# Attention with its value products cut into quarters of the query columns, and row-max products that take two spare banks in turn

## The chip, the cores and the metric

The kernel runs on one core of a Trainium2 chip. The metric is the time of one launch in device microseconds (us), the median of several runs. The profile comes from one execution taken by the hardware profiler; its engines are PE (matrix products), PEld (the loading of the stationary operand, beside PE), DVE (vector), ACT (activation functions), POOL and SP (here only an issuer of DMAs). PSUM, where matrix products land, has eight banks of 512 fp32 columns on 128 partitions; the kernel holds all eight as one tile `bk`, and `bk[:, 6]` is bank 6.

## What is computed

A gated mix of multi-head attention and of an MLP, both on the same rows:

```python
qkv = (x @ wqkv).reshape(B, S, 3, H, Dh)           # B=1, S=2048, D=448, H=16, Dh=28
scores = einsum("bhqd,bhkd->bhqk", q, k) * Dh ** -0.5
a = einsum("bhqk,bhkd->bhqd", softmax(scores), v)  # then to B,S,D and @ wo
y = layernorm(x)
b = gelu(y @ w1 + b1) @ w2 + b2                    # F = 1792
g = sigmoid((x * gate_w).sum(-1, keepdims=True))
return g * a + (1 - g) * b                         # 2048 x 448, fp32
```

## The kernel before

**Three stages.** First come the projections to queries, keys and values and the layer norm, then the MLP, both in an order that a planner with costs and due times works out (class `Strips`, its products on L472), and from about 455 us on the attention, whose order on PE is written out by hand. The change touches only the attention. Most products are split: an fp32 factor becomes a high and a low part, and three products of parts make one product of full accuracy.

**Row maxima.** The softmax subtracts a bound for each query row that comes from a pass of its own: 1024 products of 28x128 queries by 28x512 keys (`RowMax.one`, L198), each followed by a maximum over its 512 columns on DVE (L200, `mx`). Some of the 1024 are done while the planner runs; the rest are placed one by one between the products of the attention by `lone(s, b, turn)`, where `s` picks one of four heads and `b` the bank of `bk` that the product lands in. The maximum is then an additional row of the score product (29 rows instead of 28).

**Units, groups and turns.** A unit is the 128 keys x 512 queries block of one head: three score products (L1087) into one bank, an exp over the bank (L1090), and its share in a value product. A group has 64 units, 16 key tiles by 4 heads, and there are 16 groups: 4 sets of 4 heads, each with 4 chunks of 512 queries. The 1024 units are taken in turns. `turn_of(u, turn)` issues the score products and exps of one turn: five units while row maxima are owed, and six otherwise, which makes 154 turns of five, 42 of six and a last one of two. Units 0 to 2 of a turn use banks 0 to 2 and one exp (128x1536), the others banks 3, 4 (and 5) and a second exp. The exps write tiles `p0` and `p1` of a pool with three buffers each. The products run as the three parts p = 0, 1, 2 of the first half and then those of the second half. In front of some of these six places stands a `lone`: in a turn of five units in front of places 0, 3 and 5, with banks 6, 5 and 6; in a turn of six in front of 0 and 5, both with bank 6 (bank 5 then holds a unit).

**Value products.** After the scores of a turn the main loop issues value products. One batch (`batch`, L1098) is a key tile of a group: four products side by side, one per head, each of 128 keys x 32 value columns (stationary) by 128 x 512 exps, into 32 rows each of bank 7, which collects a whole group (`start` at key tile 0, `stop` at the last). One of the value columns holds ones, so that the sums of the exps come out beside the products. A batch is issued once its four units were issued in an earlier turn. With five units per turn most turns have one batch, and about every fourth has two; with six they alternate between one and two. `batch` takes an exp out of `prob` as it uses it.

**Group ends.** When a group's last batch is issued, `valued` copies bank 7 to SBUF (`finish_a`, DVE, L958), and two and four turns later the division by the sums follows (`finish_b`, `finish_c`). The batches of that turn stop there. In the last set of heads, `tail` holds the output projection of each finished 128-row tile: `project` (products on L936 to L938, bank 6; the sum with the MLP's part on DVE, `put`, L943), at most one per turn, at the end of a turn.

**Queues and agenda.** Loads and splits for the next group are put down for given turns by `at(turn, fn)` and run from `agenda` between a turn's scores and its values. Their DMAs go out on SP's and other queues, and their arithmetic goes to POOL and DVE. PE's order is that of the program text as it runs.

**The end.** After the last scores (turn 196) comes turn 197 with no scores: the first nine of the twelve projection products of one output tile in bank 6, then the value batches that are left, and `finish_last`, which closes the last group with products against `sel` (L994) and an identity (L1000) and the other projections.

Of the kernel before, what the change touches and what calls it, by code (L numbers as in the profile page):

```python
# [15 lines left out]
P = 128  # L16
# [7 lines left out]
NC = S // CH  # L24
NT = S // P
# [10 lines left out]
def kernel(ctx: ExitStack, tc: tile.TileContext, xt, wqk, wv, wo, xk, w1, b1, w2, b2,  # L36
                          ident_d, sel_d, out):
    nc = tc.nc
# [35 lines left out]
    bk = banks.tile([P, 8, CH], F32, name="bk")  # L74
# [313 lines left out]
    class Strips:  # L388
# [28 lines left out]
        def at(self, t, fn, **uses):  # L417
            self.tasks.append((t, self.count, fn, uses))
            self.count += 1
# [349 lines left out]
    khi, klo, vg = {}, {}, {}  # L769
# [87 lines left out]
    for b, m in enumerate((0, 3, 4)):  # L857
        x = QK(0, m)
# [95 lines left out]
    def finish_a(n):  # L954
        ob = ao.tile([P, CH], F32, name="ob")
        lt = ao.tile([P, CH // 32], F32, name="lt")
        obs[n] = ob, lt
        nc.vector.tensor_copy(ob, pv)  # L958
        nc.sync.dma_start(lt, ob[DH:P:32, :])

    def finish_b(n):
        ob, lt = obs[n]
        rc = ao.tile([P, CH], F32, name="rc")
        obs[n] = ob, rc
        nc.vector.reciprocal(lt, lt)
        r = rls[n]
        nc.sync.dma_start(r.rearrange("j (a b) -> (j a) b", b=CH // 32), lt)
        for j in range(4):
            nc.sync.dma_start(rc[32 * j:32 * j + 32], r[j].partition_broadcast(32))

    def finish_c(n):
        g, c = divmod(n, NC)
        ob, rc = obs.pop(n)
        if g < NG - 1:
            nc.gpsimd.tensor_mul(ot[g][:, c * CH:(c + 1) * CH], ob, rc)
            return
        nc.gpsimd.tensor_mul(ob, ob, rc)
        split_o(g, c, ob)

    def finish_last(n):  # L980

        g, c = divmod(n, NC)
        ob = ao.tile([P, CH], F32, name="ob")
        rc = ao.tile([P, CH], F32, name="rc")
        lt = ao.tile([P, CH // 32], F32, name="lt")
        h, l = (t[:, g] for t in ohs[c])
        tiles = [slice(i * P, (i + 1) * P) for i in range(TPC)]
        po = [bk[:, (6, 0, 1, 2)[i], :D] for i in range(TPC)]
        sums, ways = bk[:, 4, :NG * TPC], bk[:, 5]
        for sl in tiles:  # L990
            nc.scalar.activation(ob[:, sl], pv[:, sl], AF.Copy)
        products(po[1], c * TPC + 1, range(NG - 1))
        for i, sl in enumerate(tiles):
            nc.tensor.matmul(sums[:, NG * i:NG * i + NG], ob[:, sl], sel, start=True, stop=True)  # L994
        nc.vector.reciprocal(lt, sums)
        spread = lt.rearrange("p (i j) -> p i j", j=NG).unsqueeze(3).broadcast_to([P, TPC, NG, 32])
        nc.vector.tensor_copy(rc.rearrange("p (i j d) -> p i j d", j=NG, d=32), spread)
        products(po[2], c * TPC + 2, range(NG - 1))
        for sl in tiles:
            nc.tensor.matmul(ways[:, sl], rc[:, sl], ident, start=True, stop=True)  # L1000
        products(po[3], c * TPC + 3, range(NG - 1))
        for sl in tiles:
            nc.vector.tensor_mul(ob[:, sl], ob[:, sl], ways[:, sl])
            nc.scalar.activation(h[:, sl], ob[:, sl], AF.Copy)
            nc.vector.tensor_sub(l[:, sl], ob[:, sl], h[:, sl].bitcast(F32))
        for i in range(TPC):
            products(po[i], c * TPC + i, (NG - 1,))
            put(po[i], c * TPC + i)

    def begun(n, turn):  # L1010

        g, c = divmod(n, NC)
        if n + 1 < NG * NC:
            for j in range(4):
                at(turn + 1 + j // 2, lambda j=j: fetch_qq(n + 1, j))
            at(turn + 5, lambda: split_qq(n + 1))
            at(turn + 7, lambda: load_ms(n + 1))
        if c == (0 if g == 0 else 2) and g < NG - 1:
            for j in range(4):
                at(turn + 2 + j, lambda j=j: fetch_kk(g + 1, j))  # L1020
                at(turn + 8 + j, lambda j=j: split_kk(g + 1, j))
            at(turn + 13, lambda: key_row(g + 1))
            for t in range(2):
                at(turn + 9 + t, lambda t=t: load_v(g + 1, slice(8 * t, 8 * t + 8)))
        if g == NG - 1:
            for i in range(TPC):
                at(turn + 7 + i, lambda i=i: fetch_acc(c, i))
                at(turn + 9 + i // 2, lambda i=i: weigh_acc(c, i))
            for x in range(NG - 1):
                at(turn + 4 + x, lambda x=x: split_o(x, c, ot[x][:, c * CH:(c + 1) * CH]))  # L1030

    def valued(n, turn):

        g, c = divmod(n, NC)
        if n == NG * NC - 1:
            finish_last(n)
            return
        finish_a(n)
        at(turn + 2, lambda: finish_b(n))
        at(turn + 4, lambda: finish_c(n))  # L1040
        if g == NG - 1:
            for i in range(TPC):
                tail.append((turn + 6 + i, c * TPC + i))

    UNITS = NG * NC * 64
    prob, tail = {}, []
# [3 lines left out]
    def lone(s, b, turn):  # L1050
        if not rowmax.ready(s) or turn < cold[s]:
            return
        for kind, n, j in rowmax.one(s, bk[:, b]):
            if kind == "q":
                at(turn + 1, lambda n=n, j=j: rowmax.load_q(n, j))
            elif kind == "k":
                at(turn + 1, lambda n=n, j=j: rowmax.load_k(n, j))
                cold[j] = turn + 4
            else:
                at(turn + 1, lambda n=n: rowmax.close(n))  # L1060
                at(turn + 2, lambda n=n: rowmax.store(n))

    def turn_of(u, turn):

        left = UNITS - u
        owed = rowmax.left()
        size = min(left, 5 if owed and owed > 2 * ((left - 116) // 6) else 6)
        na, nb = min(3, size), max(0, size - 3)
        for x in range(u, u + size):
            n = x // 64  # L1070
            if n not in begins:
                begins.add(n)
                begun(n, turn)
        extra = {5: ((0, 3, 6), (3, 1, 5), (5, 2, 6)), 6: ((0, 3, 6), (5, 2, 6))}.get(size, ())
        for half, first, count in ((0, 0, na), (1, 3, nb)):
            for p in range(3):
                for x, o, b in extra:
                    if x == 3 * half + p:
                        lone((u + o) % 4, b, turn)
                for i in range(first, first + count):  # L1080
                    n, k = divmod(u + i, 64)
                    k, j = divmod(k, 4)
                    r = slice(32 * j, 32 * j + DH + (p == 0))
                    ks = slice(k * P, (k + 1) * P)
                    w = (khi, klo, khi)[p][n // NC]
                    q = (qh, qh, ql)[p][n % 3]
                    nc.tensor.matmul(bk[:, i], w[r, ks], q[r], start=(p == 0), stop=(p == 2), skip_group_check=True)  # L1087
            if count:
                t = ap.tile([P, 3, CH], F32, name=f"p{half}")
                nc.scalar.activation(t[:, :count], bk[:, first:first + count], AF.Exp, scale=SCALE)  # L1090
                for i in range(count):
                    prob[u + first + i] = t[:, i]
        return size

    def batch(b, turn):
        n, k = divmod(b, NT)
        for j in range(4):
            nc.tensor.matmul(bk[32 * j:32 * j + 32, 7], vg[n // NC][:, k, 32 * j:32 * j + 32], prob.pop(4 * b + j),  # L1098
                             start=(k == 0), stop=(k == NT - 1), skip_group_check=True)
        if k == NT - 1:  # L1100
            valued(n, turn)
            return True
        return False

    u = b = turn = 0
    while b < UNITS // 4:
        before = u
        if u < UNITS:
            u += turn_of(u, turn)
        for fn in agenda.pop(turn, ()):  # L1110
            fn()
        if turn == 0:
            for _ in range(6):
                nc.tensor.matmul(bk[:, 7], khi[0][:, 0:P], khi[0][:, 0:CH], start=True, stop=True)  # L1114
        if before == UNITS:
            products(bk[:, 6, :D], (NC - 1) * TPC, range(NG - 1))
            before = u = UNITS
        while 4 * b + 4 <= before:
            b += 1
            if batch(b - 1, turn):  # L1120
                break
        if tail and tail[0][0] <= turn:
            project(tail.pop(0)[1])
        turn += 1
# [53 lines left out]
```

## Time and profile before

| what | value |
|---|---|
| three runs | 1100.46, 1105.54, 1104.21 us; median 1104.21 us |
| profiled execution | 1101.01 us, of which the span from first to last instruction is 1099.1 us |
| mean granted clock of PE | 0.995 |
| PE busy | 1078.3 us, 98% of the span, 13153 instructions |
| PEld busy | 727.7 us, 66% |
| DVE busy | 739.7 us, 67% |
| ACT busy | 633.4 us, 58% |
| POOL busy | 362.2 us, 33% |
| PE on the chain that ended last, L472 (projections and MLP) | 33% |
| the same, L1098 (values) / L1087 (scores) / L198 (row maxima) | 21% / 18% / 14% |

How to read the rows that follow. A row of groups has the line, the engine, the operation, output <- inputs with sizes (partitions x elements), the count, then busy time and the mean duration of one in nanoseconds, and then the idle time of the engine just before these instructions with what ended it. A row of the timeline has the start in us from the span's start, the time covered, engine, line, operation, and how many instructions of the kind follow each other; in brackets stands how long the engine had been idle and what released it. Products of several heads run side by side in different parts of PE, so their durations overlap, and their ends are modelled; starts are recorded.

### The profile page before, as it was taken

Reading aid. Unit: us, or ns where it says so; the run is one execution under the profiler, and the core shown is the slowest. Engines: PE = TensorE matmul, PEld = TensorE weight load, DVE = VectorE, ACT = ScalarE, POOL = GpSimd, SP = SyncE. Lnnn points to the kernel's source line nnn. Section 1 sums busy time; section 2 is a strip of 40 time slices with the busy share of each in tenths; the row PEclk is TensorE's granted clock in tenths of the full one; section 3 lists DMA queues with packets and bytes.
Section 4 is the critical chain, followed back from the end, with each engine's and each line's share of the span. In section 5 each row is a group of like instructions: output and inputs, shape, how many; then the busy total and the mean of one; then the engine's idle time right before and its main releaser. Section 6 shows DMA issues by size and latency. Waiting matters only on the chain.

```text
span 1099.1 us, 30449 instructions
## 1 busy us (share of the span) xinstructions
PE 1078.3 (98%) x13153; PEld 727.7 (66%) x13153; DVE 739.7 (67%) x1185; ACT 633.4 (58%) x666; POOL 362.2 (33%) x372
## 2 busy tenths in 40 slices
PE   8989999999999999999999999999999999999998
PEld 5979999999999999744444444444444443454555
DVE  4169999999999999766676775676676664310102
ACT  5324264133042141387787887887887888856672
POOL 3456477535244038321101101310011214434431
PEclk9989999999999999999999999999999999999999
DMA  6685633203000105310000001400002102010211
GB/s 230 203 252 172 212 101 98 92 12 103 36 11 11 37 12 126 111 51 23 20 11 20 24 21 37 104 16 19 16 23 56 48 18 54 24 52 28 69 53 59
DMA packets 47463, 73.15 MB, mean 67 GB/s; under 512 B 13633, under 2 KB 28609, under 8 KB 46417
## 3 DMA queue, kind: packets, MB, share of 16 engines
q1 hardware_dynamic: 33888, 39.11, 12.7%
q0 software_dynamic: 4800, 16.89, 5.6%
q10 hardware_dynamic: 8640, 15.21, 3.9%
q8 instruction: 103, 1.69, 0.7%
q14 instruction: 32, 0.25, 0.1%
HBM read 51.75 MB, written 19.31 MB: 65 GB/s over the span
## 4 chain that ended last, share of the span: by engine, by line
PE 91%; ACT 3%; DMA 2%; issue 1%; POOL 1%; DVE 1%; ACTq 0%; DVEq 0%; SPq 0%; POOLq 0%
PE bk L472 33%; PE bk L1098 21%; PE bk L1087 18%; PE bk L198 14%; ACT p L1090 3%; PE bk L936 1%; PE bk L937 1%; PE bk L938 1%; PE bk L862 1%; DMA qd<-qk 1%; DMA qk<-qo 1%; POOL w1f L95 0%; DVE mx L200 0%; DMA first<-in_xt 0%; PE bk L1114 0%
## 5 line engine op out<-in xcount | busy, mean ns | idle before, releaser
L200 DVE TENSOR_REDUCE mx<-bk 128x1 f32<-128x512 f32 x1024 | 672.1, 689 | 203.2 <-PE bk L198 167.8
L1090 ACT ACTIVATE p<-bk 128x1536 f32<-128x1536 f32 (+1 forms) x393 | 481.6, 1281 | 143.9 <-PE bk L1087 137.7
L198 PE MATMUL bk<-kd,qd 28*128 28x512 f32 x1024 | 447.0, 439 | 6.1 <-DMA qd<-qk 5.2
L198 PEld LDWEIGHTS bk<-kd,qd 28*128 28x128 f32 x1024 | 186.5, 183 | 193.4 <-DVE mx L200 123.5
L472 PE MATMUL bk<-yh,w1f 32*128 32x512 f32 x1568 | 190.2, 393 | 0.1
L472 PE MATMUL bk<-yl,w1f 32*128 32x512 f32 x784 | 165.1, 390 | 0.0
L472 PEld LDWEIGHTS bk<-yh,w1f 32*128 32x128 f32 x1568 | 152.2, 183 | 2.4 <-ACT gb L382 0.8
L472 PE MATMUL bk<-w2h,hh 32*128 32x448 f32 x896 | 141.5, 366 | 0.0
L472 PE MATMUL bk<-w2l,hh 32*128 32x448 f32 x896 | 140.5, 364 | 0.1
L1098 PE MATMUL bk<-p,va 128*32 128x512 f32 x1024 | 131.2, 602 | 0.0
L1098 PE MATMUL bk<-p,vb 128*32 128x512 f32 x1024 | 129.3, 601 | 0.0
L350 POOL TENSOR_TENSOR hl<-h,hh 128x512 fp32r<-128x512 f32 x56 | 72.4, 1306 | 127.5 <-ACT hh L343 76.2
L1087 PE MATMUL bk<-yh,ka 29*128 29x512 f32 x512 | 107.8, 484 | 0.4 <-ACT gb L382 0.4
L472 PEld LDWEIGHTS bk<-yl,w1f 32*128 32x128 f32 x784 | 106.9, 183 | 0.4
L794 POOL CAST yh<-yl 128x512 fp32r<-128x512 f32 x16 | 9.8, 611 | 290.0 <-DMA yl<-qk 180.6
L472 PEld LDWEIGHTS bk<-w2l,hh 32*128 32x128 f32 x896 | 103.0, 183 | 0.7 <-DVE w2l L152 0.4
L472 PEld LDWEIGHTS bk<-w2h,hh 32*128 32x128 f32 x896 | 102.2, 183 | 0.1
L1087 PE MATMUL bk<-yh,kb 29*128 29x512 f32 x512 | 97.5, 477 | 4.1 <-ACT p L1090 4.1
L472 PE MATMUL bk<-w2h,hl 32*128 32x448 f32 x896 | 93.0, 363 | 0.0
L1087 PE MATMUL bk<-yh,la 28*128 28x512 f32 x512 | 88.8, 393 | 0.0
L1087 PE MATMUL bk<-yl,ka 28*128 28x512 f32 x512 | 87.2, 409 | 0.0
L382 ACT ACTIVATE gb<-bk 128x448 f32<-128x448 f32 x16 | 8.7, 544 | 130.2 <-PE bk L472 125.9
(137 smaller groups left out, 1593.7 us busy)
## 6 DMA issues: line engine op xcount, KB each, us to landing
qk<-qo ACTq DMA_DIRECT2D x28, 256.0 KB
raw<-in_xt SPq DMA_DIRECT2D x17, 256.0 KB
vs<-vt ACTq DMA_DIRECT2D x16, 256.0 KB
rc<-rls SPq DMA_DIRECT2D x60, 64.0 KB
bxr<-in_xk POOLq DMA_DIRECT2D x8, 448.0 KB, 6.1
gbs<-gb ACTq DMA_DIRECT2D x16, 224.0 KB
acc<-gbs SPq DMA_DIRECT2D x16, 224.0 KB
out_y<-acc SPq DMA_DIRECT2D x16, 224.0 KB
```

Of the source, the lines that this page charges most:

```text
L198: nc.tensor.matmul(ps, self.qd[n % 2][r, i * P:(i + 1) * P], self.kd[r, k * 512:(k + 1) * 512], start=True, stop=True)
L200: nc.vector.reduce_max(self.mx[n % 2][:, j, i, k:k + 1], ps, axis=AX)
L350: nc.gpsimd.tensor_sub(hl[f], h, hh[f].bitcast(F32))
L472: mm = nc.tensor.matmul(bk[:, x.bank, :n], a, b, start=x.first, stop=(len(x.rem) == 1 and m == len(ops) - 1), skip_group_check=True)
L794: nc.gpsimd.tensor_copy(h, l.bitcast(F32))
L862: nc.tensor.matmul(bk[:, b], w, v, start=(i == 0), stop=(i == len(ops) - 1), skip_group_check=True)
L936: nc.tensor.matmul(po, h, woh[:, g], start=(g == 0), stop=False, skip_group_check=True)
L937: nc.tensor.matmul(po, h, wol[:, g], start=False, stop=False, skip_group_check=True)
L938: nc.tensor.matmul(po, l, woh[:, g], start=False, stop=(g == NG - 1), skip_group_check=True)
L1087: nc.tensor.matmul(bk[:, i], w[r, ks], q[r], start=(p == 0), stop=(p == 2), skip_group_check=True)
L1090: nc.scalar.activation(t[:, :count], bk[:, first:first + count], AF.Exp, scale=SCALE)
L1098: nc.tensor.matmul(bk[32 * j:32 * j + 32, 7], vg[n // NC][:, k, 32 * j:32 * j + 32], prob.pop(4 * b + j), start=(k == 0), stop=(k == NT - ...
```

## The change

Two things are changed, both in the attention.

The function `batch` is replaced by `values(done, limit, turn)`. It counts value work in units of a quarter batch: all four heads' products over 128 of the 512 query columns of a key tile. In each turn it goes on to `limit`, which is the number of units issued before this turn less four. A batch can so be cut into pieces of 128, 256 or 384 columns, of which some belong to one turn and the others to the next; pieces that fall into one turn and one batch stay one product. The first key tile of a group (`k == 0`) is never cut. The loop still stops where a group ends. A turn has so as many quarters as a turn has units, five or six, except at the ends of groups, behind them, and at the start. The exps are no longer taken out of `prob`.

The banks of the row-max products are taken by a counter: in turns of five units they alternate between 6 and 5 from one product to the next, across turns too. In turns of six all go to bank 6, as before. Places and heads of the row-max products are unchanged.

In the changed program there are 1536 value products instead of 1024: 512 of 512 columns, 288 of 384, 448 of 256 and 288 of 128. The scores stand on L1090, their exp on L1093, the value products on L1106; L198, L200, L936 to L943 and L958 keep their numbers.

```diff
     def lone(s, b, turn):
         if not rowmax.ready(s) or turn < cold[s]:
             return
+        lone.count += 1
         for kind, n, j in rowmax.one(s, bk[:, b]):
...
+    lone.count = 0
+
     def turn_of(u, turn):
...
-        extra = {5: ((0, 3, 6), (3, 1, 5), (5, 2, 6)), 6: ((0, 3, 6), (5, 2, 6))}.get(size, ())
+        extra = {5: ((0, 3), (3, 1), (5, 2)), 6: ((0, 3), (5, 2))}.get(size, ())
         for half, first, count in ((0, 0, na), (1, 3, nb)):
             for p in range(3):
-                for x, o, b in extra:
+                for x, o in extra:
                     if x == 3 * half + p:
-                        lone((u + o) % 4, b, turn)
+                        lone((u + o) % 4, 6 - lone.count % 2 if size == 5 else 6, turn)
...
-    def batch(b, turn):
-        n, k = divmod(b, NT)
-        for j in range(4):
-            nc.tensor.matmul(bk[32 * j:32 * j + 32, 7], vg[n // NC][:, k, 32 * j:32 * j + 32], prob.pop(4 * b + j),
-                             start=(k == 0), stop=(k == NT - 1), skip_group_check=True)
-        if k == NT - 1:
-            valued(n, turn)
-            return True
-        return False
-
-    u = b = turn = 0
-    while b < UNITS // 4:
+    def values(done, limit, turn):
+
+        while done < limit:
+            b, lo = divmod(done, 4)
+            n, k = divmod(b, NT)
+            hi = min(4, lo + limit - done) if k else 4
+            cs = slice(lo * P, hi * P)
+            for j in range(4):
+                nc.tensor.matmul(bk[32 * j:32 * j + 32, 7, cs], vg[n // NC][:, k, 32 * j:32 * j + 32], prob[4 * b + j][:, cs],
+                                 start=(k == 0), stop=(k == NT - 1), skip_group_check=True)
+            done += hi - lo
+            if hi == 4 and k == NT - 1:
+                valued(n, turn)
+                break
+        return done
+
+    u = done = turn = 0
+    while done < UNITS:
         before = u
...
         if before == UNITS:
             products(bk[:, 6, :D], (NC - 1) * TPC, range(NG - 1))
-            before = u = UNITS
-        while 4 * b + 4 <= before:
-            b += 1
-            if batch(b - 1, turn):
-                break
+        done = values(done, before if before == UNITS else before - 4, turn)
         if tail and tail[0][0] <= turn:
             project(tail.pop(0)[1])
```

## The prediction

> **What bounds the kernel now.** I read the page first (shares, chain), then the groups by shape for durations, then the timeline of the attention stage turn by turn. From the page:
>
> ```profile
> span 1099.1 us, 30449 instructions
> ...
> PE 1078.3 (98%) x13153; PEld 727.7 (66%) x13153; DVE 739.7 (67%) x1185; ACT 633.4 (58%) x666; POOL 362.2 (33%) x372
> ...
> PE 91%; ACT 3%; DMA 2%; issue 1%; POOL 1%; DVE 1%; ACTq 0%; DVEq 0%; SPq 0%; POOLq 0%
> ...
> L1098 PE MATMUL bk<-p,va 128*32 128x512 f32 x1024 | 131.2, 602 | 0.0
> ```
>
> PE carries 91% of the chain, so the change acts only through PE: through the work of L1098 (the value products, 2 x 1024 records with `vb`), or through what PE waits for. A busy PE says little here, since its ends are modelled. I therefore use starts. The attention stage is a series of 197 turns from 455 us on: 154 take five units (query chunk, key tile, head), 42 take six. Here are four five-unit turns, beginning at 704.32, 707.89, 710.59 and 713.29:
>
> ```profile
> 704.32 0.50 PE L198 MATMUL bk<-kd,qd 28*128 28x512 f32 x1
> ...
> 706.03 1.92 PE L1098 MATMUL bk<-p,vb 128*32 128x512 f32 x16
> ...
> 707.89 0.49 PE L198 MATMUL bk<-kd,qd 28*128 28x512 f32 x1
> ...
> 708.42 0.69 DVE L200 TENSOR_REDUCE mx<-bk 128x1 f32<-128x512 f32 x1 [1.56 <-PE bk L198]
> ...
> 708.98 2.37 ACT L1090 ACTIVATE p<-bk 128x1536 f32<-128x1536 f32 x2 [1.21 <-PE bk L1087]
> 709.16 0.18 PEld L198 LDWEIGHTS bk<-kd,qd 28*128 28x128 f32 x1 [0.27 <-DVE mx L200]
> ...
> 709.59 1.07 PE L1098 MATMUL bk<-p,vb 128*32 128x512 f32 x8
> ...
> 710.59 0.49 PE L198 MATMUL bk<-kd,qd 28*128 28x512 f32 x1
> ...
> 711.39 0.49 PE L1087 MATMUL bk<-yh,kb 29*128 29x512 f32 x1
> ...
> 713.29 0.49 PE L198 MATMUL bk<-kd,qd 28*128 28x512 f32 x1
> ...
> 716.00 0.49 PE L198 MATMUL bk<-kd,qd 28*128 28x512 f32 x1
> ```
>
> A turn is scores (1.70: 707.89 to 709.59), then values. One batch of values takes 1.00 (709.59 to 710.59), two take 1.86 (706.03 to 707.89), so a quarter of a batch costs (1.86 - 1.00) / 4 = 0.215 and the section has 0.14 beside it. The four turns take 11.68, or 2.92 on average, with one double in them.
>
> Two waits stand at the edge. (a) The exp pair ends at 708.98 + 2.37 = 711.35 and the second half of the next scores starts at 711.39, 0.80 into its turn: exp releases it. (b) The third row-max product of a turn (709.16) waits for the reduction of the first (708.42 + 0.69 = 709.11), 1.27 into the turn. Where the first is absent, scores take 1.58 instead of 1.70:
>
> ```profile
> 696.21 0.53 PE L1087 MATMUL bk<-yh,kb 29*128 29x512 f32 x4
> ...
> 697.79 0.64 PE L1098 MATMUL bk<-p,vb 128*32 128x512 f32 x4
> ```
>
> So either wait alone costs 0.12, and the turn that begins at 707.89, after a double, shows it: exp was done long before, and scores still took 1.70, by (b).
>
> **The change, part by part.**
>
> *Plain five-unit turns.* 129 turns of the changed program get exactly five quarters, in two pieces (2+3, 1+4, 4+1, 3+2). Values: 0.14 + 5 x 0.215 = 1.21. Wait (a) goes: the exp pair ends 711.35 - 707.89 = 3.46 into its turn, the next half is wanted at 2.91 + 0.80 = 3.71. Wait (b) stays: products now alternate between the two spare banks, and the third again uses the bank of the first. What is late next is therefore (b), and scores stay at 1.70. A turn is 2.91 against 2.92: 0. What the alternation does remove is the first product's wait for the third one of the turn before; that reduction starts at 708.42 + 2 x 0.69 = 709.80 or later and ends by 710.5, before 710.59, and value sections are equally long before every such turn. Worth 0. Bounds for the group: 0.02 a turn either way, 2.6 in all; the 0.12 of (b) is a rival.
>
> *Pieces.* 1024 value matmuls become 1536; four heads run side by side and each matmul makes two passes, so 256 passes more, with a weight load each. The columns stay the same. The nearest rows are the short plain products at the end and the weight load of L1098:
>
> ```profile
> 1088.64 1.05 PE L1000 MATMUL bk<-ident,rc 128*128 128x128 f32 x8
> ...
> 1089.45 0.45 PE L936 MATMUL bk<-woh,oh 128*128 128x448 f32 x1
> ```
> ```profile
> L198 PEld LDWEIGHTS bk<-kd,qd 28*128 28x128 f32 x1024 | 186.5, 183 | 193.4 <-DVE mx L200 123.5
> ```
> ```profile
> L1098 PEld LDWEIGHTS bk<-p,va 128*32 128x32 f32 x728 | 16.2, 108 | 28.8 <-issue 28.8
> ```
>
> Eight passes of 128 columns, each with its own load, take 0.81, 0.101 each; half of 0.215 is 0.107. So short passes cost no more than their share: I take 0. A gain is excluded, as no column goes. The upper bound is a load wholly exposed per pass: 256 x 0.108 = 27.6.
>
> The Trainium skill speaks against the change here. Its page "TensorE: Matmul & The Clock Gate", section "Back-to-back issue gap", gives 81 ns per matmul of 128 columns in a stream of load-and-matmul pairs where streaming alone would be 56, which is 25 ns for each small matmul. By it, as an estimate, 256 passes would add 6.4 and the sum below would be 8.1. The trace does not agree: 0.101 a pass with the load in it.
>
> *Group ends.* A group is 64 units, a turn five, and the value section breaks off at a group's end. Before, that costs little; what it shows is the copy of the result, which holds up the row-max reduction:
>
> ```profile
> 725.07 0.50 PE L198 MATMUL bk<-kd,qd 28*128 28x512 f32 x1
> ...
> 725.28 0.69 DVE L958 COPY ob<-bk 128x512 f32<-128x512 f32 x1 [0.39 <-PE bk L1098]
> ...
> 727.05 0.63 PE L1098 MATMUL bk<-p,vb 128*32 128x512 f32 x3
> ```
>
> Scores there take 1.98. The copy remains. But now a group's last turn holds 5, 4, 3, 2 or only 1 quarter, and the arrears follow: 7, 8 or 9 in the next. After a 1-quarter turn (1.70 + 0.35 = 2.05) exp ends 3.46 - 2.05 = 1.41 into the next one instead of at most 0.80, and from there 0.04 and 0.90 (711.39 to the next values, as 708.69 to 709.59) lead to values at 2.35 or, as exp itself is pushed, 2.5: 0.5 over 1.98. In that turn a new wait shows: the arrears still read the exp tiles of three turns ago, whose buffers the exp of this turn wants. In the changed program this exp waits for the first value piece of its own turn (2.5 + 0.86 and some 0.2 of matmul tail: 3.6 instead of 1.4). PE queues the next scores behind that exp. It ends at 3.6 + 2.37 = 6.0, the next turn begins at 2.5 + 0.14 + 9 x 0.215 = 4.6, so its second half starts at 1.4 instead of 0.80: another 0.65. This happens twice (2 x 1.2). Twice a 2-quarter end costs 0.3, three 3-quarter ends 0.1 each, and the start-up, where values begin with 4 and then 2 quarters, 0.4. Net of small items: +3.4. Bounds: 0, if arrears meet slack I do not see; 7 at double.
>
> 71 exps of the second half in all wait for a value piece. In plain turns it is 1 or 2 quarters: values at 1.70 plus 0.43 and a tail of 0.17 give 2.3, while exp's turn comes at 708.98 - 707.89 + 1.35 = 2.44 (pitch of two exps from the rows below). That is hidden by the first exp; the cover fails by 0.25 at least before anything moves (3.46 against 3.71).
>
> *Six-unit turns.* Two of them:
>
> ```profile
> 938.04 0.49 PE L198 MATMUL bk<-kd,qd 28*128 28x512 f32 x1
> ...
> 939.12 2.79 ACT L1090 ACTIVATE p<-bk 128x1536 f32<-128x1536 f32 x2 [1.18 <-PE bk L1087]
> ...
> 939.76 1.06 PE L1098 MATMUL bk<-p,vb 128*32 128x512 f32 x8
> ...
> 940.75 0.50 PE L198 MATMUL bk<-kd,qd 28*128 28x512 f32 x1
> ...
> 941.97 0.50 PE L1087 MATMUL bk<-yh,kb 29*128 29x512 f32 x3 [0.24 <-ACT p L1090]
> ...
> 942.87 1.92 PE L1098 MATMUL bk<-p,vb 128*32 128x512 f32 x16
> ...
> 944.72 0.49 PE L198 MATMUL bk<-kd,qd 28*128 28x512 f32 x1
> ```
> ```profile
> 960.19 0.51 PE L1087 MATMUL bk<-yh,kb 29*128 29x512 f32 x3
> ...
> 962.43 0.64 PE L1098 MATMUL bk<-p,vb 128*32 128x512 f32 x4
> ```
>
> (The exp pair of 2.79 with 1.45 for the last puts the pitch near 1.35.) The short turn runs ahead of exp and the long one pays: scores 2.12 instead of 1.70, and 2.24 instead of 1.60 where no row-max is left. By the timeline six turns pay 0.42 and eight 0.64: 7.6. With 6 quarters each turn is 1.70 + 0.14 + 1.29 = 3.13; exp ends 1.08 + 2.79 = 3.87 into it, the next half is wanted at 3.13 + 0.80 = 3.93. So most of it goes. Where no row-max is left the turn is 3.03 and every second one still pays 0.2; two group ends (1 and 2 quarters, then 10 and 10) pay 1.9 and 1.3. About 4.9 remains: -2.7. Bounds: -5 and 0.
>
> *The end.* Values lag four units, so the last group but one ends a turn later, and its last projection comes to stand right before the closing products, in the same bank 6:
>
> ```profile
> 1078.77 0.37 PE L938 MATMUL bk<-woh,ol 128*128 128x448 f32 x1
> 1079.06 0.50 PE L1087 MATMUL bk<-yh,kb 29*128 29x512 f32 x2
> 1079.23 0.69 DVE L943 SCALAR_TENSOR_TENSOR acc<-bk,gate,acc 128x448 f32<-128x448 f32 x1 [5.42 <-PE bk L938]
> ```
>
> Now scores and values lie between them and hide L943. Without these, PE waits from about 1078.98 to 1079.23 + 0.69 + 0.05: +1.0. The value work moved to the end replaces what was done earlier on a busy PE: 0.
>
> **Sum.** 0 + 0 + 3.4 - 2.7 + 1.0 = +1.7. The profiled execution took 1101.01 (span 1099.1 and 1.9 around it), so it would become 1102.7. It lies 3.2 below the median of the three runs, 1104.21; on the median I add the same 1.7: **1105.9**.
>
> **Rivals.**
>
> 1. *Small pieces pay (slower).* Place: the 144 passes of 128 columns in the value sections. For it: four heads must be loaded in the 0.107 of one pass, and a load lasts 0.108, that of L198 even 0.183. Against: 0.101 in L1000. At 0.15 a pass, between the two loads: 144 x 0.043 = 6.2, time 1112.1; at 0.183, 1116.8. The Trainium skill's rule above points the same way. It makes a slower kernel by 5.5 from (5.5 - 1.7) / 144 = 0.026 a pass, that is from 0.133.
> 2. *The new exp waits decide (slower).* If the 71 exps were released only at the end of the value section, at 2.91 instead of 2.44, they would end at 3.93, 0.22 past 3.71: +16, time 1122. Against: the wait names the first piece.
> 3. *Wait (b) yields too (faster).* If with (a) gone the third row-max product came early enough in plain turns, scores fall to 1.58: 129 x 0.12 = -15.5, time 1090.4. Against: the turn at 707.89 had no (a) and took 1.70.
>
> **How the numbers follow.** About 0.5%, 5.5 us, is what a measurement of this kernel tells from no change. Forecast 0.48 (no change; its own range, from the bounds of group ends, plain turns and six-unit turns, 1100 to 1110); rival 1: 0.32, rival 2: 0.05, rival 3: 0.15. Slower is 0.37, faster 0.15. The range 1099 to 1117 takes in the forecast and rival 1 up to its dearer end (and 1 below the forecast's own range, for the spread of the runs) and leaves out rivals 2 and 3, 0.20.
>
> **What would show it.** Plain turns of 2.91 with scores of 1.70 and values of 1.21, whichever way they are cut; a third row-max product still waiting at 1.27; six-unit scores of 1.6 to 1.8 instead of 2.24; after two or three group ends an exp that waits for L1106 and scores of 2.3 or more in two turns running; a stop of about 1.0 before the closing products. Values of a 1+4 turn longer than those of a 3+2 turn by over 0.06 speak for rival 1, exps that start after 2.5 in plain turns for rival 2, plain scores under 1.65 for rival 3. I am wrong if the time leaves 1099 to 1117, or if it stays inside with plain turns that are not 2.91.

## The result and the profile after

| | before | changed |
|---|---|---|
| median (range) of 12 runs each | 1102.34 us (1099.42 to 1105.54) | 1107.08 us (1103.17 to 1110.26) |
| profiled execution, span / clock | 1099.1 us / 0.995 | 1101.9 us / 0.992 |
| ratio of times, 95% interval | 1 | 1.004 (1.0022 to 1.0057) |

The kernel became 4.7 us slower, a little within the 0.5% that the prediction called no change; 1.7 more were forecast. The interval leaves out 1, so the loss is small but real. The page's chain looks much as before. Here it is by line before, then by engine and by line after (L1090 was the exp before and is the scores now):

```profile
PE bk L472 33%; PE bk L1098 21%; PE bk L1087 18%; PE bk L198 14%; ACT p L1090 3%; PE bk L936 1%; PE bk L937 1%; PE bk L938 1%; PE bk L862 1%; DMA qd<-qk 1%; DMA qk<-qo 1%; POOL w1f L95 0%; DVE mx L200 0%; DMA first<-in_xt 0%; PE bk L1114 0%
```
```profile
PE 93%; DMA 2%; ACT 2%; POOL 1%; DVE 1%; issue 1%; SPq 0%; ACTq 0%; DVEq 0%; POOLq 0%
PE bk L472 33%; PE bk L1106 21%; PE bk L1090 18%; PE bk L198 16%; PE bk L936 1%; ACT p L1093 1%; PE bk L938 1%; PE bk L937 1%; PE bk L862 1%; DMA qd<-qk 1%; POOL w1f L95 0%; DVE mx L200 0%; DMA first<-in_xt 0%; DMA rls<-lt 0%; DMA kd<-qk 0%
```

Exp's share fell from 3% to 1%, and the row-max products (L198) took what it left: 16% instead of 14%. Two DMAs at the end of the row are new. The timeline of three plain turns (start, time covered, engine, line) shows why nothing came of the shorter wait:

```profile
550.26 0.49 PE L198 MATMUL bk<-kd,qd 28*128 28x512 f32 x1
...
551.53 0.50 PE L198 MATMUL bk<-kd,qd 28*128 28x512 f32 x1
551.97 1.28 PE L1106 MATMUL bk<-p,va 128*32 128x128 f32 x16
553.18 0.49 PE L198 MATMUL bk<-kd,qd 28*128 28x512 f32 x1
...
554.46 0.49 PE L198 MATMUL bk<-kd,qd 28*128 28x512 f32 x1
554.89 1.28 PE L1106 MATMUL bk<-p,va 128*32 128x512 f32 x16
556.10 0.50 PE L198 MATMUL bk<-kd,qd 28*128 28x512 f32 x1
...
557.82 1.28 PE L1106 MATMUL bk<-p,va 128*32 128x384 f32 x16
559.03 0.50 PE L198 MATMUL bk<-kd,qd 28*128 28x512 f32 x1
```

The turns take 2.92, 2.92 and 2.93, and the third row-max product still starts 1.27 and 1.28 into the first two. Scores take 1.71 or 1.72 and values 1.21, whichever way the five quarters are cut. Wait (a) did go, and it shows where wait (b) is absent: in two neighbouring turns that have only two row-max products each, scores took 1.58 and 1.81 before (from 696.21 and 698.79; the second half of the latter starts at 699.70, when the exp pair of 697.28 has ended at 699.65) and take 1.59 and 1.59 now.

Now the turns where the third group ends (counted from 0 it is group 2), by the timeline, with DVE's copy and ACT's exps:

```profile
575.37 0.42 PE L1106 MATMUL bk<-p,va 128*32 128x128 f32 x8
575.73 0.49 PE L198 MATMUL bk<-kd,qd 28*128 28x512 f32 x1
576.10 0.68 DVE L958 COPY ob<-bk 128x512 f32<-128x512 f32 x1
...
578.05 2.14 PE L1106 MATMUL bk<-p,va 128*32 128x512 f32 x24
579.20 2.37 ACT L1093 ACTIVATE p<-bk 128x1536 f32<-128x1536 f32 x2 [2.10 <-PE bk L1106]
580.12 0.50 PE L198 MATMUL bk<-kd,qd 28*128 28x512 f32 x1
...
582.51 1.28 PE L1106 MATMUL bk<-p,va 128*32 128x384 f32 x16
```

The first of these turns has one quarter (575.37). The next has scores of 2.32 (575.73 to 578.05), nine quarters, and an exp that waited 2.10 for a value product and starts 3.47 into the turn. The one after that has scores of 2.39 (580.12 to 582.51). This is the group-end story of the prediction. What it had not seen is in the turn that begins at 701. The chain there (start, us, what), and then the row-max product in the timeline:

```profile
695.17 3.52 DMA rls<-lt
...
698.71 0.31 SPq L969
...
700.50 0.36 SPq L184
...
700.90 3.21 DMA kd<-qk
```
```profile
704.25 0.47 PE L198 MATMUL bk<-kd,qd 28*128 28x512 f32 x1 [2.27 <-DMA kd<-qk]
```

The sums of a group are stored (`rls<-lt`), SP waits until that landed, issues four broadcasts of them (L969), and only then the loads of queries and keys for the row maxima (L184, L178). The keys land 3.21 later, and the row-max product that stands in front of PE's queue waits 2.27 for them: that turn's scores take 4.15 instead of 1.72. Before, the same group ended one turn earlier, and so did these DMAs, by the timeline of SP's issues:

```profile
692.67 0.35 SPq L967 DMA_DIRECT2D rls<-lt  x1
694.95 1.69 SPq L969 DMA_DIRECT2D rc<-rls  x4
...
697.19 0.33 SPq L184 DMA_DIRECT2D qd<-qk  x1
697.57 0.37 SPq L178 DMA_DIRECT2D kd<-qk  x1
```

A second new wait follows the six-unit turn of 914.41:

```profile
918.34 0.50 PE L198 MATMUL bk<-kd,qd 28*128 28x512 f32 x1 [0.92 <-ACT p L1093]
```

The counter gave this five-unit turn's first row-max product bank 5, in which the six-unit turn before it had a unit; so it waits for that unit's exp. Before, the first product of every turn went to bank 6.

The stretch before the first value product varies from execution to execution (it starts at 461.96 in the profile of before, at 460.96 in that of after, at 467.44 in one of the experiments), and of the change only the first two turns' row-max banks lie in it. Where profiles are compared below, I take the time from that start to the end of the span, called the attention stage: before 1099.1 - 461.96 = 637.1, after 1101.9 - 460.96 = 640.9.

### The profile page after: what moved, and what is told of

It reads as the page before. It is cut to its first block, busy times and chain, and to the rows that moved or that the text cites. A ratio compares the mean times of both kernels' runs of the same rounds, so it can differ in the third digit from the quotient of the medians.

```text
span 1101.9 us, 32503 instructions
## 1 busy us (share of the span) xinstructions
PE 1079.8 (98%) x14177; PEld 754.4 (68%) x14177; DVE 738.7 (67%) x1185; ACT 635.7 (58%) x666; POOL 362.4 (33%) x372
## 3 DMA queue, kind: packets, MB, share of 16 engines
q8 instruction: 111, 1.82, 0.7%
## 4 chain that ended last, share of the span: by engine, by line
PE 93%; DMA 2%; ACT 2%; POOL 1%; DVE 1%; issue 1%; SPq 0%; ACTq 0%; DVEq 0%; POOLq 0%
PE bk L472 33%; PE bk L1106 21%; PE bk L1090 18%; PE bk L198 16%; PE bk L936 1%; ACT p L1093 1%; PE bk L938 1%; PE bk L937 1%; PE bk L862 1%; DMA qd<-qk 1%; POOL w1f L95 0%; DVE mx L200 0%; DMA first<-in_xt 0%; DMA rls<-lt 0%; DMA kd<-qk 0%
## 5 line engine op out<-in xcount | busy, mean ns | idle before, releaser
L200 DVE TENSOR_REDUCE mx<-bk 128x1 f32<-128x512 f32 x1024 | 671.6, 688 | 211.9 <-PE bk L198 179.2
L1093 ACT ACTIVATE p<-bk 128x1536 f32<-128x1536 f32 (+1 forms) x393 | 483.8, 1281 | 142.5 <-PE bk L1090 126.5
L198 PE MATMUL bk<-kd,qd 28*128 28x512 f32 x1024 | 446.4, 440 | 8.4 <-DMA qd<-qk 4.7
L198 PEld LDWEIGHTS bk<-kd,qd 28*128 28x128 f32 x1024 | 186.4, 183 | 149.4 <-DVE mx L200 103.1
L1106 PE MATMUL bk<-p,va 128*32 128x512 f32 (+3 forms) x1600 | 131.6, 445 | 0.0
L1106 PE MATMUL bk<-p,vb 128*32 128x512 f32 (+3 forms) x1472 | 129.6, 469 | 0.0
L1090 PE MATMUL bk<-yh,ka 29*128 29x512 f32 x512 | 115.8, 479 | 0.7 <-ACT gb L382 0.5
L1090 PE MATMUL bk<-yh,kb 29*128 29x512 f32 x512 | 100.3, 477 | 1.2 <-ACT p L1093 0.9
L1090 PE MATMUL bk<-yh,la 28*128 28x512 f32 x512 | 94.8, 396 | 0.0
L1090 PE MATMUL bk<-yl,ka 28*128 28x512 f32 x512 | 93.2, 432 | 0.0
L1090 PE MATMUL bk<-yh,lb 28*128 28x512 f32 x512 | 82.5, 392 | 0.0
```

Of the source, the lines that this page charges most:

```text
L198: nc.tensor.matmul(ps, self.qd[n % 2][r, i * P:(i + 1) * P], self.kd[r, k * 512:(k + 1) * 512], start=True, stop=True)
L200: nc.vector.reduce_max(self.mx[n % 2][:, j, i, k:k + 1], ps, axis=AX)
L1106: nc.tensor.matmul(bk[32 * j:32 * j + 32, 7, cs], vg[n // NC][:, k, 32 * j:32 * j + 32], prob[4 * b + j][:, cs], start=(k == 0), stop=(k = ...
```

## The experiments

**The changed kernel again, and its two halves alone.** The first is unchanged. In the second the row-max products keep their banks:

```diff
-        extra = {5: ((0, 3), (3, 1), (5, 2)), 6: ((0, 3), (5, 2))}.get(size, ())
+        extra = {5: ((0, 3, 6), (3, 1, 5), (5, 2, 6)), 6: ((0, 3, 6), (5, 2, 6))}.get(size, ())
...
-                        lone((u + o) % 4, 6 - lone.count % 2 if size == 5 else 6, turn)
+                        lone((u + o) % 4, b, turn)
```

In the third the kernel before gets the reverse of these lines, with the counter that they need, and nothing else.

> The changed kernel once more, beside the others on one chip. Theory (what its first trace showed beside the forecast): a row-max product waits 2.3 us for a load of keys in the turn that begins at 701, since the group that ends there ends one turn later than before and its DMAs now stand on SP's queue ahead of that load; and the first row-max product of the turn after a six-unit turn waits 1.0 for an exp, since the alternation gives it bank 5. Both are fixed by the program's order, so both come again, within 0.3. Rival: the 2.3 was a chance delay of one execution, and here the turn takes 1.7 for its scores like its neighbours. Ratio to before 1.002 to 1.006.

Measured: 1106.96 us, ratio 1.0038 (1.0024 to 1.0052). Both waits came again: scores of 3.96 in the turn at 701, and 0.9 behind the six-unit turn. They belong to the program's order. Attention stage 640.7.

> The value products are cut as in the change, the row-max products keep their old banks (6, 5, 6 in each turn). Theory: in plain turns the alternation is worth nothing, since the reduction of a turn's third product ends some 0.15 before the next turn: scores 1.70, values 1.21, turn 2.92 as with the alternation. Only the wait of 1.0 behind the six-unit turn goes, so 1.0 less than the changed kernel, about 1106. Rival: without the alternation the first product of a turn waits for the third of the turn before; 0.05 or more in each of about 135 turns, that is 7 or more above the changed kernel, 1114.

Measured: 1105.68 us, ratio 1.0022 (1.0007 to 1.0037). Plain turns have the same 1.71 and 1.21, and the wait behind the six-unit turn is gone, as the theory had it. One thing it had not: after a turn with a single quarter the first row-max product now does wait for the third of the turn before (value section 0.87 instead of 0.36), and the next scores are shorter by as much (1.81 instead of 2.32): the alternation moved a wait there and saved nothing. The stop for the keys is there too, with a second long turn behind it (scores 4.23 and 2.86); its size differs between executions. In this profile the granted clock of PE is 0.5 from 711.3 to 718.1, just behind the stop, and the three turns from 706 on take 14.2 where the changed kernel's take 11.2; in the profile of the changed kernel the clock stays at 1.0 behind it.

> The old whole batches, with the alternating banks. Theory: worth nothing in plain turns, costs the wait of 1.0 in one turn behind a six-unit turn: 0 to 2 above the kernel before, ratio 1.000 to 1.002. Rival: in the short turns (2.70) the alternation frees the first product and they become shorter by 0.05 or more: 115 turns, 6 below the kernel before, ratio 0.995.

Measured: 1103.78 us, ratio 1.0005 (0.9991 to 1.0019). Plain turns are unchanged (1.71, 1.00 and 1.85); the value section of the one six-unit turn concerned is 2.18 instead of 1.00, and the next scores are 1.71 instead of 2.07. The alternation alone brings nothing; by the trace it costs 0.8, which the times can't tell from 0.

**Group ends without arrears.**

```diff
-        done = values(done, before if before == UNITS else before - 4, turn)
+        end = 64 * (done // 64 + 1)
+        limit = before if before == UNITS else before - 4
+        if limit < end <= min(before, limit + 3):
+            limit = end
+        done = values(done, limit, turn)
```

> The change, but where three quarters or fewer of a group are left over behind a turn's quota, the turn does them too (their units were issued in earlier turns). So no group ends with a turn of 1 to 3 quarters and none is followed by arrears. Theory: the arrears cost what the trace shows over a plain group end with its copy (scores 1.98): 0.16 + 0.35 + 0.69 + 0.15 + 0.52 + 0.69 + 0.35 + 0.62 + 0.27 = 3.8 in the nine turns concerned, and the 2.4 in the turn at 701 goes with them, as that group ends a turn earlier again: 6 less than the changed kernel, about 1101. Rival: group ends cost nothing, the difference lies in the plain turns and their small pieces; then it stays at 1107.

Measured: 1099.03 us (1097.75 to 1099.39), ratio to before 0.996 (0.9946 to 0.9973). It is faster than both kernels: 7.9 below the changed one on the same chip, against 6 expected, and 4.3 below the kernel before. Attention stage 633.7, so 7.0 to 7.3 below the two profiles of the changed kernel. The group end that was shown above, in its timeline:

```profile
574.86 1.50 PE L1106 MATMUL bk<-p,va 128*32 128x256 f32 x16
576.28 0.50 PE L198 MATMUL bk<-kd,qd 28*128 28x512 f32 x1
576.49 0.69 DVE L958 COPY ob<-bk 128x512 f32<-128x512 f32 x1 [0.80 <-PE bk L1106]
...
578.26 1.07 PE L1106 MATMUL bk<-p,va 128*32 128x512 f32 x8
579.26 0.50 PE L198 MATMUL bk<-kd,qd 28*128 28x512 f32 x1
...
580.97 1.28 PE L1106 MATMUL bk<-p,va 128*32 128x512 f32 x16
```

The last turn of the group has six quarters, then comes the copy with scores of 1.98, then four quarters, scores of 1.71, and five quarters. The keys come in time as well (scores of 1.71 in the turn concerned). What I had not counted: the last group but one ends a turn earlier again, so the wait before the closing products (0.83) is gone too.

**Wait (b) made short, in both kernels.** The first row-max product of a five-unit turn is reduced over 128 columns only (the last line as the changed kernel has it):

```diff
-            nc.vector.reduce_max(self.mx[n % 2][:, j, i, k:k + 1], ps, axis=AX)
+            nc.vector.reduce_max(self.mx[n % 2][:, j, i, k:k + 1], ps[:, :width], axis=AX)
...
-                        lone((u + o) % 4, 6 - lone.count % 2 if size == 5 else 6, turn)
+                        lone((u + o) % 4, 6 - lone.count % 2 if size == 5 else 6, turn, 128 if size == 5 and x == 0 else 512)
```

> The changed kernel, but in five-unit turns the first of the three row maxima is taken over 128 of its 512 columns (part of the maximum is left out). So the bank that the third product needs is free some 0.5 earlier. Theory: the third product's wait for that reduction (wait b) is all that holds scores at 1.70, since the split took the wait for exp (wait a) away. Scores fall to 1.58 in some 140 turns: 16 less, about 1091. Rival: something else holds them too (exp again, or the products themselves), and scores stay at 1.65 or more: 1100 or more.

> The same shortening of the first row maximum in the kernel before (part of the maximum is left out). Theory: both waits stood there side by side, so taking only wait (b) away leaves the wait for exp in the turns of one batch: of four turns two stay at 1.70 and two fall to 1.58 (the turn behind a double, and the one that follows a turn that had waited), some 70 turns by 0.12: 8 less than before, about 1094, and 3 or more above the changed kernel with the same edit. Rival: exp never held anything, and the gain is the same 16 as with the split: 1086.

Measured: 1094.19 us with the split (ratio to before 0.9916, 0.9896 to 0.9936), 1097.96 without it (0.9953, 0.9934 to 0.9971). Both timelines, the one with the split first:

```profile
505.58 0.50 PE L198 MATMUL bk<-kd,qd 28*128 28x512 f32 x1
506.12 0.29 DVE L200 TENSOR_REDUCE mx<-bk 128x1 f32<-128x128 f32 x1 [0.33 <-PE bk L198]
506.40 0.56 PE L198 MATMUL bk<-kd,qd 28*128 28x512 f32 x2
...
507.18 1.28 PE L1106 MATMUL bk<-p,va 128*32 128x512 f32 x16
508.39 0.50 PE L198 MATMUL bk<-kd,qd 28*128 28x512 f32 x1
```
```profile
519.12 0.49 PE L198 MATMUL bk<-kd,qd 28*128 28x512 f32 x1
...
520.72 1.07 PE L1098 MATMUL bk<-p,va 128*32 128x512 f32 x8
521.71 0.50 PE L198 MATMUL bk<-kd,qd 28*128 28x512 f32 x1
...
523.52 1.06 PE L1098 MATMUL bk<-p,va 128*32 128x512 f32 x8
524.51 0.50 PE L198 MATMUL bk<-kd,qd 28*128 28x512 f32 x1
```

With the split all plain scores fall to 1.60 (505.58 to 507.18). Without it they alternate between 1.60 (519.12 to 520.72) and 1.81 (521.71 to 523.52): a short turn runs ahead of exp, and the next one waits for it (the exp pair that starts at 520.20 ends at 522.57, and the second half of the scores at 522.62), 1.70 on the mean. That the wait costs 0.21 in every second turn is more than I had put (0.12 in two of four, and two at 1.58). So the kernel before gains little in plain turns (0.01 each); most of what its attention stage gains (632.7, so 4.4) lies at group ends, where the row-max products are held up by the copy. With wait (b) short, the split makes the kernel faster by 3.8 (1097.96 to 1094.19, one chip), although its arrears and its stop for the keys are still in. With wait (b) as it is, it makes it slower by about 4.

**Smaller pieces.** Each piece is cut again, to 128 columns, and to 64:

```diff
-            cs = slice(lo * P, hi * P)
-            for j in range(4):
...
+            for e in range(lo * P, hi * P, 128):
+                cs = slice(e, e + 128)
+                for j in range(4):
...
```

> The changed kernel, with every value product cut into pieces of 128 columns, 4096 instead of 1536. Theory: a pass of 128 columns costs its share of a longer one; five quarters take 1.21 however cut, and the time stays within 2 of the changed kernel. Rival (small pieces pay): at 0.15 a pass instead of 0.107, 1280 more short passes cost 0.043 each: 55 more, 1162.

> The same with pieces of 64 columns, 8192 products. Theory: a pass then streams for 0.054, while the loads of its four heads last 0.108: if the loads of one pass can't hide behind more than one pass before, five quarters take 0.14 + 20 x 0.108 = 2.3 instead of 1.21 and the kernel about 1107 + 205 x 1.1 = 1330. Rival: loads of several passes run beside each other and nothing is paid, 1107.

Measured: 1109.54 us (ratio to before 1.0055, 1.0035 to 1.0075) and, in a single run, 1126.54. Five quarters take 1.23 as five pieces and 1.25 as ten, against 1.21 as two: 5 ns for each further piece of four products. The groups by shape of the kernel with 64 columns:

```profile
L1107 PE MATMUL bk<-p,vb 128*32 128x64 f32 x8192 | 138.8, 221 | 3.7 <-issue 3.6
...
L1107 PEld LDWEIGHTS bk<-p,vb 128*32 128x32 f32 x8192 | 121.5, 110 | 34.1 <-issue 33.4
```

8192 loads of 110 ns each have a busy time of 121.5 us, a seventh of their sum (901): they run beside each other, the four heads' and more than one pass's, which is why they hide even behind a pass of some 54 ns (an estimate, half of the 0.107 for 128 columns). Rival 1 is out. The kernel with 64 columns does lose 23 in its attention stage (663.6), of which 1664 further pieces at 5 ns make 8. The rest are, beside 3.4 us at a granted clock of 0.5 behind the stop for the keys, single stops, mostly inside value sections, like this one in its timeline:

```profile
983.80 0.44 PE L1107 MATMUL bk<-p,vb 128*32 128x64 f32 x17
985.28 0.32 PE L1107 MATMUL bk<-p,vb 128*32 128x64 f32 x7 [1.04 <-issue]
```

PE waited there for nothing that the trace shows. The page counts 3.52 MB of instructions loaded, against 1.82 with the change as it is; that PE ran out of instructions would fit, but no run shows it.

**The loads first.** A group's broadcasts, so far the second half of `finish_b`, get a function of their own and are issued one turn after the store of its sums, and the row maxima's loads come first in a turn:

```diff
+    def spread(n):
...
         at(turn + 2, lambda: finish_b(n))
+        at(turn + 3, lambda: spread(n))
...
-                at(turn + 1, lambda n=n, j=j: rowmax.load_k(n, j))
+                agenda.setdefault(turn + 1, []).insert(0, lambda n=n, j=j: rowmax.load_k(n, j))
```

(`load_q` likewise.)

> The changed kernel, but the loads of queries and keys for the row maxima come first among a turn's DMAs, and the broadcasts of a group's sums, which wait on SP for the store of the sums to land, are issued one turn later than that store. Theory: the wait of 2.3 in the turn that begins at 701 is the load standing behind those broadcasts (issued at 700.9, 3.7 after the store); ahead of them it lands in time, that turn's scores take 1.7 instead of 4.0 to 4.2, and the kernel 2.4 less, about 1104.6, with a narrower spread. Rival: the load's own way from issue to landing is what lasts, or its readers hold it up; then the turn stays above 3.

Measured: 1103.19 us (1101.38 to 1106.44), ratio to before 1.0006 (0.9992 to 1.0021). SP's issues in its timeline:

```profile
691.58 0.33 SPq L178 DMA_DIRECT2D kd<-qk  x1
691.96 0.38 SPq L184 DMA_DIRECT2D qd<-qk  x1
...
695.80 0.35 SPq L964 DMA_DIRECT2D rls<-lt  x1
...
698.93 1.70 SPq L972 DMA_DIRECT2D rc<-rls  x4
```

The keys' load now stands ahead of the store, and the turn's scores take 1.72. The attention stage is 638.8, so 2.0 less; the medians, from different chips, differ by 3.8 (ratios 1.0038 and 1.0006). The clock is a likely reason for the difference. The two profiled runs of the changed kernel were among the fastest of their twelve (1103.87 and 1103.56), and their clock stayed at 1.0 behind the stop; in the profiles of e1, e5, e7 and e8 it is 0.5 there, for 6.8, 3.4, 3.4 and 3.4 us. The mean granted clock of all runs fits: 0.9917 and 0.9921 in the two series of the changed kernel, 0.9947 here, and 0.9941 to 0.9945 in the runs of the kernel before beside the experiments. For a single run without a profile it isn't shown.

**Both odd waits out as well.** The kernel without arrears, and:

```diff
+        lone.count += size == 5 and turn_of.last == 6 and lone.count % 2
+        turn_of.last = size
...
-            products(bk[:, 6, :D], (NC - 1) * TPC, range(NG - 1))
+            products(bk[:, 3, :D], (NC - 1) * TPC, range(NG - 1))
...
-        po = [bk[:, (6, 0, 1, 2)[i], :D] for i in range(TPC)]
+        po = [bk[:, (3, 0, 1, 2)[i], :D] for i in range(TPC)]
```

> e3_ends, and in addition: the first row-max product behind a six-unit turn takes bank 6 again, and the closing products use bank 3 instead of bank 6, so that they don't follow a projection in the same bank. Theory: the wait of 1.0 behind the six-unit turn goes and the stop of 0.83 before the closing products too: 1.8 below e3_ends, about 1097.2, ratio to before 0.9944. Rival: other engines end at the same time there (ACT behind the six-unit turn, the sums of the last group at the end), and 0.5 or less is gained.

Measured: 1098.64 us, ratio to before 0.9961 (0.9943 to 0.9978); attention stage 633.4. No gain that can be told from e3_ends. The wait before the closing products had gone already, as said above, so one of the two edits had nothing to act on; behind the six-unit turn 0.78 went (2.21 to 1.43) and 0.27 came back in the next scores (1.71 to 1.98).

**A quarter of the values in the gap of wait (b).** That kernel, and in five-unit turns, ahead of the third row-max product:

```diff
...
+                if size == 5 and 3 * half + p == 5 and turn_of.done % 64 in range(4, 63) and turn_of.done < u - 4:
+                    turn_of.done = values(turn_of.done, turn_of.done + 1, turn)
...
```

> e10_best, and in five-unit turns one quarter of the turn's value products stands ahead of the third row-max product, inside the scores. Theory: the third product then comes at about 1.37 instead of 1.15 and the reduction it waits for ended at 1.27, so the wait of 0.12 is filled with work: turns of 2.80 instead of 2.92, some 135 of them, 16 less, about 1081. Rival: the 0.14 that a value section has beside its quarters is the price of going from score products to value products and back, and is paid twice in such a turn: 2.93 or more, 1099 or more.

Measured: 1131.01 us, ratio to before 1.0253 (1.0227 to 1.0279). One turn in its timeline:

```profile
562.73 0.49 PE L198 MATMUL bk<-kd,qd 28*128 28x512 f32 x1
...
564.09 0.43 PE L1112 MATMUL bk<-p,va 128*32 128x128 f32 x8
564.45 0.50 PE L198 MATMUL bk<-kd,qd 28*128 28x512 f32 x1
564.45 0.50 PE L1094 MATMUL bk<-yl,ka 28*128 28x512 f32 x2
564.88 1.06 PE L1112 MATMUL bk<-p,va 128*32 128x512 f32 x8
565.88 0.50 PE L198 MATMUL bk<-kd,qd 28*128 28x512 f32 x1
```

A turn takes 3.15 (562.73 to 565.88) instead of 2.92: the rival came, and it was dearer than it said. The inserted quarter takes 0.36 (564.09 to 564.45) where 0.215 is its share, and the scores' two parts take 1.36 + 0.43 = 1.79, 0.08 more than with the wait of 0.12 in them. So one more change from score products (28 or 29 rows of PE) to value products (all 128 rows, 32 columns) and back costs 3.15 - 2.92 = 0.23 even with a wait of 0.12 to fill. In the 140 turns with an inserted quarter that makes 32, which is what this kernel lies above the one without it (1098.64). The page "TensorEngine Tiling (Array Packing)" of the Trainium skill, section "Key Properties", says that a change of the tiling mode drains the engine; this trace agrees, with the 0.23, though no run tells a drain from another cost of the change.

## Why the prediction was right

It forecast no change, with 1.7 more, in 1099 to 1117; 4.7 more were measured. By its own steps, in the attention stage of the two profiles (3.8 apart):

| step | forecast | measured |
|---|---|---|
| plain five-unit turns: wait (a) goes, (b) stays | 0 | 0: 2.92, third product at 1.27 |
| pieces | 0 | +0.6: values 1.214, where before (3 x 0.996 + 1.854) / 4 = 1.2105; 0.0035 x 154 and some 0.0025 x 40 |
| bank alternation | 0 | +1.0, behind one six-unit turn |
| group ends and start-up | +3.4 | +1.4: scores of the other turns before the first six-unit turn 260.60 against 259.25 |
| six-unit turns, with two group ends | -2.7 | -2.7: scores from the first six-unit turn on 76.88 against 79.60 |
| the end | +1.0 | +0.8 |
| DMAs of a group end moved past the load of the keys | not seen | +2.4 |
| sum | +1.7 | +3.5 |

Of the 0.3 that is left, 0.2 is an exp that the scores behind a group end wait for (value section from 1042.35, 0.79 instead of 0.57).

*Plain turns.* The step on which the sign hung was that two equal waits stood side by side. e5 and e6 show it: shorten (b), and the split is worth 0.10 in each plain turn. It was right that the turn at 707.89, with no wait for exp, had to be believed. What it had of wait (a) by itself was too simple, as e6's pattern of 1.60 and 1.81 shows.

*Group ends.* The mechanism was right in detail: scores of 2.32 and 2.39 where 2.5 and about 2.35 were put, the exp at 3.47 into its turn where 3.6 was, and e3 proves that the arrears cost what the trace says. The term came out smaller because four turns of the kernel before (one of them at 545.41, scores of 1.98) are shorter with the split, 1.74 to 1.77; e1, with the split alone, has 1.77 there, e2 1.97. Five more turns with one or two row-max products, where wait (a) stood alone, are 0.5 shorter together. That relief was the slack which the lower bound allowed for; the arrears themselves, with the start-up, cost 2.9.

*Rival 1* had the largest chance of the three and fell: by it e7 would have cost 55, and it cost 2.6 by the medians of one chip and 3.8 in the attention stage (644.7), of which 1.1 is the value section at half clock behind the stop for the keys. From the 81 and 56 ns of the Trainium skill ("TensorE: Matmul & The Clock Gate", "Back-to-back issue gap") the prediction had an estimate of 6.4 for the change; 0.6 was measured, in a place where four heads' products and loads run side by side. *Rival 2* didn't come: plain turns kept their 2.92 with the new waits in them. *Rival 3* fell as forecast, and e5 shows what it would have been worth.

*What was missed.* The prediction moved group ends by a turn for PE and bank 7, but not their DMA steps on SP's queue, and these meet the load of the keys at one of fifteen group ends. And the alternation was looked at in plain turns, where it is worth nothing, and not at the border behind a six-unit turn, where the counter's parity picks a bank that is taken. Together they are 3.4 of the 3.8. That the time still came out only 1.2 above the 1105.9 that was forecast is in part luck: the group ends cost 2.0 less than was put, and the forecast started from a median of three runs that lies 1.9 above that of twelve.

## What to carry to other kernels

Where two waits end at the same place, taking one away shows nothing: look for a turn in the trace in which one of them is already absent, and shorten the other before judging an edit. Work that is smoothed over turns needs a rule for where its groups end: here a line that lets a turn finish three quarters more turned a loss of 0.4% into a gain of 0.4%. And when a step moves by a turn, go through every queue that it issues to; a DMA that waits on its queue for another to land holds up all that stands behind it.

## What the runs showed of the hardware

A value piece of four side-by-side products costs some 5 ns beside its columns, down to 64 columns, since loads overlap several deep (110 ns each, 8192 in 121.5 us of busy time). One more change from score to value products and back cost a turn 0.23 us net, far more than a cut within one kind. The store of a group's sums took 2.3 us before and 3.5 after from its issue to that of the broadcasts behind it on SP's queue. Behind a stop of PE for the keys of 1.5 to 2.4 us the granted clock stayed at 1.0 in two profiles and was 0.5 for 3.4 or 6.8 us in four.
